# Letting the output matmuls of two token blocks take turns in the two halves of a PSUM bank

## The chip, the cores and the metric

The kernel runs on one core of one Trainium2 chip. The metric is the device time of one execution in microseconds; most executions of one kernel agree within 0.3%. A trace belongs to one profiled execution, whose span is some 2 us shorter than the timed execution (695.1 us of 696.8 us for the kernel before). It gives the start of every matmul; the ends of matmuls in it are modelled, so lengths and busy times of matmuls below carry that model, and spacings of starts don't.

## The reference

The first half is a short causal convolution along the tokens, with softmax weights of 7 taps per head. The second half is a two-layer network with a Swish activation. Only the second half matters here.

```python
# x: 32768 tokens x 192, w_in: 192 x 2048, w_out: 2048 x 192
def _moe_ref(x, w_in, w_out, beta):
    h = x @ w_in
    g = h * (1.0 / (1.0 + np.exp(-beta * h)))
    return (g @ w_out).astype(np.float32)
```

## The kernel before

Two halves of the batch are processed at once, one in partitions 0 to 63 and one in partitions 64 to 127. A step takes 512 tokens of each half. It has 16 rounds, and in one round TensorE does two things. It computes one group of 128 hidden features for the current step ("hidden", three pairs of matmuls), and it does one sixteenth of the output matmuls of the previous step ("output", eight pairs).

A *pair* is two matmuls, one per row half of the array (rows 0 to 63 and 64 to 127), which run at the same time. Each writes a bank of its own in PSUM, the memory that matmuls write and in which their sums add up. The stationary operand is loaded into the array first (LDWEIGHTS, listed as PEld); the moving operand then streams through it, column by column. For the output, the stationary operand is a 64 x 128 piece of the activations `g` (64 features of 128 tokens), and the moving operand is a 64 x 192 piece of `w_out_s`. Sixteen pairs (`fc` from 0 to 15) add up to one block of 128 tokens. Two blocks share a PSUM tile: block 0 (`b == 0`) lies in columns 0 to 191 of each bank, block 1 in columns 192 to 383. When both are done, VectorE (DVE) copies one bank, adds the other, and the result is stored.

```python
    def output(s, u):
        g = gs[s]
        nb = steps[s][2] // BLK
        per = 2 * nb
        for i in range(u * per, (u + 1) * per):
            blk, fc = divmod(i, NF)               # all 16 fc of one block, then the next block
            h, q = divmod(blk, nb)
            b = q % 2
            single = s == N_ST - 1 and h == 1 and q >= nb - 2
            if single:
                b = 0
            if fc == 0 and b == 0:
                state["po"] = psum_o.tile([128, 2, TOK], FP32, name="po")
            # ... (osb tile)
            for r in range(2):                    # the two row halves: one pair
                rows = slice(r * 64, (r + 1) * 64)
                nc.tensor.matmul(
                    po[:, r, b * D : (b + 1) * D],
                    g[rows, fc, h, q * BLK : (q + 1) * BLK],   # stationary
                    w_out_s[rows, fc, :],                      # moving
                    start=(fc == 0),
                    stop=(fc == NF - 1),
                )
            if fc == NF - 1 and (b == 1 or single):
                # ... copy po[:, 0], add po[:, 1], store
```

## Time and profile before

| | before |
|---|---|
| median of the timed runs | 697.0 us (3 runs, 696.14 to 697.85) |
| TensorE busy share of the span | 99% |
| ScalarE / VectorE busy share | 83% / 80% |
| start of one output pair to start of the next | 82.5 ns |
| start of one hidden pair to start of the next | 215.8 ns |

These are lines of the profile's page of the kernel before: the span, the busy time of each engine (share of the span, number of instructions), the chain of work that ended last by engine, and the costliest groups. A group's columns are the line, engine, operation, output<-inputs, shapes and count, then busy us and mean ns of one, then the idle time of the engine just before them.

```profile
span 695.1 us, 24857 instructions
...
PE 686.9 (99%) x11465; PEld 525.9 (76%) x11465; DVE 553.2 (80%) x935; ACT 578.7 (83%) x545; POOL 69.8 (10%) x83
...
PE 96%; DVE 3%; ACT 0%; issue 0%
...
L370 ACT ACTIVATE g<-ph,beta 128x1024 bf16<-128x1024 f32 (+1 forms) x528 | 571.8, 1088 | 97.0 <-PE ph L363 93.1
L410 PEld LDWEIGHTS <-g 64*128 64x128 bf16 x8192 | 368.9, 94 | 102.4 <-issue 0.2
L410 PE MATMUL po<-w_out_s,g 64*128 64x192 bf16 x8192 | 429.8, 243 | 0.0
L363 PE MATMUL ph<-ct,w_in_s 64*128 64x512 bf16 (+1 forms) x3168 | 425.5, 370 | 2.8 <-ACT g L370 1.4
```

TensorE (PE) is busy all the time and is 96% of the chain. The output matmuls have 0.0 us of idle time in front of them. A mean of 243 ns is the length of one matmul from its start to its modelled end. It is not the price of one, because matmuls overlap: 8,192 of 243 ns would be 1,991 us.

The windows view of the same kernel shows three stretches of the steady part. Each entry is the busy time in that stretch with the number of instructions; then come the granted clock, the DMA share and GB/s.

```profile
core 0: us, PE busy (x) PEld busy (x) DVE busy (x) ACT busy (x) POOL busy (x), PEclk, DMA share, GB/s
60.00:260.00 200.00, 200.00 (x3371) 152.88 (x3367) 175.60 (x297) 170.32 (x154) 30.68 (x34) 1.00 0.92 101
260.00:460.00 200.00, 200.00 (x3371) 152.88 (x3368) 162.70 (x279) 170.44 (x153) 0.00 (x0) 1.00 0.25 60
460.00:660.00 200.00, 200.00 (x3370) 152.88 (x3366) 152.37 (x257) 170.48 (x153) 0.00 (x0) 1.00 0.20 54
```

TensorE is busy in every nanosecond of 600 us at full clock. To learn the price of a pair one needs starts. The timeline of two rounds (start in us, busy us, engine, group, count) shows the rhythm:

```profile
start us, us, engine line op out<-in xcount [idle before <-releaser]
...
400.31 0.83 PE L363 MATMUL ph<-ct,w_in_s 64*128 64x512 bf16 x6
...
400.96 0.84 PE L410 MATMUL po<-w_out_s,g 64*128 64x192 bf16 x16
401.17 1.11 ACT L370 ACTIVATE g<-ph,beta 128x1024 bf16<-128x1024 f32 x1 [0.19 <-PE ph L363]
...
401.62 0.83 PE L363 MATMUL ph<-ct,w_in_s 64*128 64x512 bf16 x6
...
402.92 0.83 PE L363 MATMUL ph<-ct,w_in_s 64*128 64x512 bf16 x6
```

Hidden runs start at 400.31, 401.62 and 402.92 us: a round takes about 1.305 us. ScalarE (ACT) takes 1.11 us of it and then waits 0.19 us for TensorE, so ScalarE follows and does not lead. The starts of single matmuls are read from the trace's records. Around 400 us they are, for the output:

```
399649  399668   399731  399750   399814  399833   399896  399915  (ns)
```

Each two are a pair. The partner starts 19 ns after the first, and the next pair 63 or 64 ns after that. Between 60 and 550 us the mean from pair to pair is 82.50 ns over 5,242 spacings inside output runs (counted on each row half), and none of them is outside 82 to 83 ns. Hidden pairs have 215.84 ns. Three hidden and eight output pairs are 3 x 215.8 + 8 x 82.5 = 1,307 ns, which is the whole round.

### The profile page before, as it was taken

How to read it: one execution, taken by the hardware profiler on the slowest of the kernel's cores; microseconds unless marked ns; L12 is line 12 of the kernel's file. 1: busy time of each engine (PE TensorE's matmuls, PEld its weight loads, DVE VectorE, ACT ScalarE, POOL GpSimd, SP SyncE). 2: the span in 40 equal slices, each digit the busy share in tenths (PEclk: the TensorE clock that was granted, in tenths of full speed). 3: DMA queues.
4: the chain of work that ended last, by engine and by line, in shares of the span. 5: the costliest groups of instructions: out<-in, count | busy, mean ns of one | idle time of the engine just before them, and what ended most of it. 6: DMA issues, size and time to landing. Idle time of an engine off the chain costs nothing.

```text
span 695.1 us, 24857 instructions
## 1 busy us (share of the span) xinstructions
PE 686.9 (99%) x11465; PEld 525.9 (76%) x11465; DVE 553.2 (80%) x935; ACT 578.7 (83%) x545; POOL 69.8 (10%) x83
## 2 busy tenths in 40 slices
PE   8899999999999999999999999999999999999997
PEld 6767777777777777777777777777777777777777
DVE  6999999998777987777987777987778987777222
ACT  5898888888888888888888888888888888888881
POOL 6934455000000000000000000000000000000000
PEclk9999999999999999999999999999999999999999
DMA  9999999922232022322023222032123122111012
GB/s 175 146 160 160 169 177 171 138 62 70 54 65 71 27 68 72 47 70 70 26 70 71 49 70 69 26 71 70 48 72 55 41 70 71 48 48 48 25 48 70
DMA packets 181497, 54.57 MB, mean 79 GB/s; under 512 B 146432, under 2 KB 181072, under 8 KB 181392
## 3 DMA queue, kind: packets, MB, share of 16 engines
q0 software_dynamic: 98048, 14.89, 29.9%
q1 hardware_dynamic: 83296, 38.09, 23.6%
q8 instruction: 89, 1.46, 0.9%
q14 instruction: 16, 0.13, 0.1%
q10 hardware_dynamic: 48, 0.01, 0.0%
HBM read 28.98 MB, written 37.29 MB: 95 GB/s over the span
## 4 chain that ended last, share of the span: by engine, by line
PE 96%; DVE 3%; ACT 0%; issue 0%
PE po L410 48%; PE ph L363 46%; DVE ct L346 2%; DVE ct L344 1%; PE ph L204 1%; PE ph L249 0%; PE po L236 0%; PE po L208 0%; DVE w_in_s L149 0%; ACT g L370 0%; PE po L249 0%; DVE xt L314 0%; DVE osb L425 0%; DVE ct L300 0%; DVE osb L424 0%
## 5 line engine op out<-in xcount | busy, mean ns | idle before, releaser
L370 ACT ACTIVATE g<-ph,beta 128x1024 bf16<-128x1024 f32 (+1 forms) x528 | 571.8, 1088 | 97.0 <-PE ph L363 93.1
L410 PEld LDWEIGHTS <-g 64*128 64x128 bf16 x8192 | 368.9, 94 | 102.4 <-issue 0.2
L410 PE MATMUL po<-w_out_s,g 64*128 64x192 bf16 x8192 | 429.8, 243 | 0.0
L363 PE MATMUL ph<-ct,w_in_s 64*128 64x512 bf16 (+1 forms) x3168 | 425.5, 370 | 2.8 <-ACT g L370 1.4
L346 DVE SCALAR_TENSOR_TENSOR ct<-xt,cw,ct 128x512 bf16<-128x512 bf16 x558 | 380.4, 746 | 0.0
L363 PEld LDWEIGHTS <-w_in_s 64*128 64x128 bf16 x3168 | 162.4, 94 | 56.9 <-issue 3.6
L424 DVE COPY osb<-po 128x384 f32<-128x384 f32 x127 | 70.8, 558 | 126.3 <-PE po L410 120.2
L425 DVE TENSOR_TENSOR osb<-po,osb 128x384 f32<-128x384 f32 x129 | 71.5, 554 | 6.0 <-ACT osb L422 1.6
L95 POOL DMA_DIRECT2D xd<-in_x_dram x60 | 54.3, 906 | 47.8 <-DMA xd<-in_x_dram 43.5
L344 DVE TENSOR_SCALAR ct<-xt,cw 128x512 bf16<-128x512 bf16 x93 | 31.6, 393 | 0.0
L422 ACT COPY osb<-po 128x192 f32<-128x192 f32 x2 | 0.6, 318 | 9.9 <-PE po L410 9.9
L320 POOL TENSOR_TENSOR w_out_s<-w_out_raw,beta_r 128x768 bf16<-128x768 f32 x4 | 5.9, 1500 | 2.3 <-DMA w_out_raw<-in_moe_w_out_dram 2.3
L204 PE MATMUL ph<-zeros 128*128 128x512 bf16 x8 | 3.8, 627 | 1.3 <-DVE warm L132 1.3
L249 PE MATMUL po<-xt_145,diag 128*128 128x256 f32 x28 | 4.4, 296 | 0.0
L249 PEld LDWEIGHTS po<-xt_145,diag 128*128 128x128 f32 x28 | 3.6, 189 | 0.7 <-issue 0.6
L149 DVE COPY w_in_s<-w_in_s 64x1536 bf16<-64x1536 bf16 x4 | 2.7, 699 | 1.5 <-DMA w_in_s<-in_moe_w_in_dram 1.4
L184 POOL DMA_DIRECT2D w_out_raw<-in_moe_w_out_dram x4 | 3.1, 782 | 0.0
L249 PEld LDWEIGHTS ph<-xt_145,diag 128*128 128x128 f32 x14 | 2.6, 269 | 0.7 <-ACT xt_145 L270 0.6
L249 PE MATMUL ph<-xt_145,diag 128*128 128x256 f32 x14 | 3.1, 375 | 0.0
L204 PEld LDWEIGHTS <-zeros 128*128 128x128 bf16 x8 | 0.9, 130 | 2.5 <-issue 1.3
L142 POOL DMA_DIRECT2D w_in_s<-in_moe_w_in_dram x4 | 2.6, 667 | 0.8 <-POOLq L479 0.8
L261 ACT CAST ct<-po 128x256 bf16<-128x256 f32 x1 | 0.4, 372 | 2.8 <-PE po L249 2.8
(46 smaller groups left out, 27.7 us busy)
## 6 DMA issues: line engine op xcount, KB each, us to landing
out_dram<-osb SPq DMA_DIRECT2D x60, 384.0 KB, 3.0
xd<-in_x_dram POOLq DMA_DIRECT2D x54, 198.0 KB, 14.6
w_out_raw<-in_moe_w_out_dram POOLq DMA_DIRECT2D x4, 384.0 KB, 9.6
out_dram<-osb SPq DMA_DIRECT2D x7, 192.0 KB, 3.8
xd<-in_x_dram POOLq DMA_DIRECT2D x6, 192.0 KB, 14.0
x_83<-in_x_dram SPq DMA_DIRECT2D x4, 192.0 KB, 3.9
w_in_s<-in_moe_w_in_dram POOLq DMA_DIRECT2D x4, 192.0 KB, 7.9
xt<-xd SPq DMA_TRANSPOSE x30, 4.6
```

Of the source, the lines that this page charges most:

```text
L95: nc.gpsimd.dma_start(out=xd[r0:, :, h, :], in_=x_v[p, t0:t1, h, :].rearrange("t (c d) -> t c d", c=NG),)
L184: nc.gpsimd.dma_start(out=w_out_raw[:, c : c + 4, :], in_=w_out_v[:, c : c + 4, :])
L204: nc.tensor.matmul(pf[:, 0, :], zeros[:, 0:128], zeros, start=True, stop=True)
L249: nc.tensor.matmul(pv, diag[:, c, k, :], xt0[:, c, o : o + n], start=(k == 0), stop=(k == K - 1),)
L320: nc.gpsimd.tensor_tensor(w_out_s[:, c0 : c0 + n, :], w_out_raw[:, c0 : c0 + n, :], beta_r[:, c0 : c0 + n].unsqueeze(2).to_broadcast((128, ...
L344: nc.vector.tensor_scalar_mul(dst, src, scalar)
L346: nc.vector.scalar_tensor_tensor(out=dst, in0=src, scalar=scalar, in1=dst, op0=ALU.mult, op1=ALU.add)
L363: nc.tensor.matmul(ph[:, h, 0:n], w_in_s[rows, j, cols], cts[s][rows, j, 0:n], start=(j == 0), stop=(j == NG - 1),)
L370: nc.scalar.activation(gs[s][:, fc, :, 0:n], ph[:, :, 0:n], AF.Silu, scale=beta[:, fc : fc + 1])
L410: nc.tensor.matmul(po[:, r, b * D : (b + 1) * D], g[rows, fc, h, q * BLK : (q + 1) * BLK], w_out_s[rows, fc, :], start=(fc == 0), stop=(fc ...
L424: nc.vector.tensor_copy(dst, po[:, 0, cols])
L425: nc.vector.tensor_tensor(dst, po[:, 1, cols], dst, ALU.add)
```

## The change

Its evident intent is to separate successive accumulations. Before, each output matmul adds onto the columns that the matmul just before it in the same row half has written. With turns, block 0 and block 1 alternate, so a column is written again only every second pair. Successive pairs then also share the moving operand `w_out_s[rows, fc]`. `start` marks a matmul that begins a new sum; one without it adds. Because a PSUM bank now holds two open sums, only the first matmul of block 0 may have `start` set. The last two blocks of the program keep the old order, since they are copied and stored one by one.

```diff
--- before.py
+++ after.py
@@ -393,9 +393,14 @@
         nb = steps[s][2] // BLK
         per = 2 * nb
         for i in range(u * per, (u + 1) * per):
-            blk, fc = divmod(i, NF)
-            h, q = divmod(blk, nb)
-            b = q % 2
+            pair, rest = divmod(i, 2 * NF)
+            h, q = divmod(2 * pair, nb)
+
+            if s == N_ST - 1 and h == 1 and q == nb - 2:
+                b, fc = divmod(rest, NF)
+            else:
+                fc, b = divmod(rest, 2)
+            q += b
 
             single = s == N_ST - 1 and h == 1 and q >= nb - 2
             if single:
@@ -411,8 +416,9 @@
                     po[:, r, b * D : (b + 1) * D],
                     g[rows, fc, h, q * BLK : (q + 1) * BLK],
                     w_out_s[rows, fc, :],
-                    start=(fc == 0),
+                    start=(fc == 0 and b == 0),
                     stop=(fc == NF - 1),
+                    skip_group_check=True,
                 )
             if fc == NF - 1 and (b == 1 or single):
                 n_q = 1 if single else 2
```

## The prediction

> **What bounds the kernel now.** TensorE. The busy table gives PE 99% of the 695.1 us span, ACT 83%, DVE 80%; the chain of waits puts 96% on PE, 48% on output matmuls. The windows view has PE busy 200.00 of 200.00 us in three windows between 60 and 660 us, at granted clock 1.00. Matmuls overlap, so "busy" proves little; I read start times. In a steady round (timeline near 400 us) output matmuls come in pairs, one per row half: the partner starts 19 to 20 ns later, the next pair 63 to 64 ns after that, so a pair costs 82.5 ns; a hidden pair costs 215.8 ns. A round of 3 hidden and 8 output pairs is 3 x 215.8 + 8 x 82.5 = 1307 ns; rounds in the timeline start every 1.30 to 1.31 us. From 60 to 660 us no gap between output starts exceeds 64 ns, nor any other 197 ns: nothing waits.
>
> **Is there a stall to remove?** The change separates consecutive accumulations into the same PSUM columns: today each 192-column matmul adds onto what its row half wrote 82.5 ns earlier. A stall there would make the pair longer than its streaming. The Trainium skill, "TensorE: Matmul & The Clock Gate", section "Back-to-back issue gap", gives N/2.4 + 2.5 ns: 82.5 ns for N = 192, 215.8 ns for N = 512. The trace agrees to a tenth of a nanosecond. So accumulation costs nothing that turns could hide. Even if the 2.5 ns beyond streaming vanished from all 4,096 output pairs, it would be 10 us (1.5%); the hidden pairs show the same 2.5 ns, so I expect none.
>
> **What it removes, adds, moves.** No operation is removed or added. In the compiled orders DVE, ACT, POOL and SP match row by row in operation and wait; on PE only operands are reordered within each 32-pair group, and four waits (two for scaled output weights, two for the last activations) move later. Weight loads stay 8,192 of 94 ns, hidden behind the previous pair: the shared moving operand saves none, as g is the stationary one. A PSUM tile completes at the same place, so copies, adds and stores keep their times. The last two blocks keep their order, so the tail (last matmul at 690.7 us to the end) stays. The moved waits cost nothing: output matmuls show 0.0 us of idle.
>
> **Correctness.** Only block 0's first matmul has start set. The skill, "PSUM — Partial Sum Buffer", section "The four PSUM rules", says that this clears the written-bits of the whole bank, so block 1's first matmul overwrites. No run here shows it yet.
>
> **On the critical path.** All output matmuls are, but their change is estimated as 0 ns. Prediction: 697.0 us, range 695.0 to 699.2 (the three runs spread 696.1 to 697.9). Chances: faster by over 2% 0.01, within 2% 0.97, slower by over 2% 0.02.
>
> **What would show the steps right or wrong.** Right: output pairs 82.5 ns apart, rounds of 1.305 us, output matmul mean 243 ns, weight loads 94 ns, the other engines' groups unchanged, PE without idle. Wrong: pair spacing near 80 ns (a hidden accumulation cost) or above 83 ns (alternating columns or weight addresses cost something), or a new PE wait on DVE or ACT.
>
> **What would make it wrong.** A cost of switching columns inside a bank, or of weight reads that jump between token blocks: each nanosecond per pair adds 4 us, so 3.4 ns leaves the 2% band. A gain beyond 2% needs a pair under 79.1 ns, less than its 80 ns of streaming.

## The result

No change of the time could be measured.

| | before | after |
|---|---|---|
| median | 696.57 us (4 runs, 696.0 to 697.85) | 696.94 us (4 runs, 696.36 to 697.1) |
| ratio | 1 | 1.0001 (95% interval 0.9984 to 1.0019) |
| output pair to output pair, mean | 82.50 ns | 82.50 ns |
| hidden pair to hidden pair, mean | 215.84 ns | 215.82 ns |
| start of the last matmul to the end of the span | 4.37 us | 4.36 us |

The median before is 696.57 us here and 697.0 us above because a fourth run was added.

The lines of the page of the kernel after that answer to those above (its output matmuls stand at another line of the file, L415):

```profile
span 695.4 us, 24857 instructions
...
PE 687.2 (99%) x11465; PEld 527.5 (76%) x11465; DVE 552.5 (79%) x935; ACT 578.7 (83%) x545; POOL 69.8 (10%) x83
...
PE 94%; DVE 3%; DMA 1%; POOL 1%; issue 0%; ACT 0%; POOLq 0%
...
L370 ACT ACTIVATE g<-ph,beta 128x1024 bf16<-128x1024 f32 (+1 forms) x528 | 571.8, 1088 | 97.0 <-PE ph L363 93.0
L415 PEld LDWEIGHTS <-g 64*128 64x128 bf16 x8192 | 369.7, 94 | 101.4
L415 PE MATMUL po<-w_out_s,g 64*128 64x192 bf16 x8192 | 430.2, 243 | 0.0
L363 PE MATMUL ph<-ct,w_in_s 64*128 64x512 bf16 (+1 forms) x3168 | 426.0, 370 | 2.8 <-ACT g L370 1.4
```

The three stretches of the kernel after:

```profile
core 0: us, PE busy (x) PEld busy (x) DVE busy (x) ACT busy (x) POOL busy (x), PEclk, DMA share, GB/s
60.00:260.00 200.00, 200.00 (x3368) 153.31 (x3366) 174.98 (x296) 170.32 (x154) 31.02 (x35) 1.00 0.93 101
260.00:460.00 200.00, 200.00 (x3369) 153.31 (x3366) 162.72 (x279) 170.43 (x154) 0.00 (x0) 1.00 0.25 60
460.00:660.00 200.00, 200.00 (x3370) 153.26 (x3366) 152.42 (x258) 170.42 (x154) 0.00 (x0) 1.00 0.21 54
```

And its timeline:

```profile
400.61 0.83 PE L363 MATMUL ph<-ct,w_in_s 64*128 64x512 bf16 x6
...
401.26 0.84 PE L415 MATMUL po<-w_out_s,g 64*128 64x192 bf16 x16
401.48 1.11 ACT L370 ACTIVATE g<-ph,beta 128x1024 bf16<-128x1024 f32 x1 [0.19 <-PE ph L363]
...
401.92 0.83 PE L363 MATMUL ph<-ct,w_in_s 64*128 64x512 bf16 x6
...
403.23 0.83 PE L363 MATMUL ph<-ct,w_in_s 64*128 64x512 bf16 x6
```

The starts of single output matmuls in this stretch, again from the trace's records:

```
401262  401282   401344  401364   401427  401447   401509  401529  (ns)
```

Counts are the same, and means, idle times and the period of a round (400.61, 401.92, 403.23 us) are the same too. Pairs are 82 or 83 ns apart as before. The chain has 94% instead of 96% on TensorE. This difference lies in the first 15 us: after, the chain runs through 8 us of loading the input weights there, and before through TensorE's first work. A second profile of the changed kernel has 96% again, so it is no effect of the change.

### The profile page after: what moved, and what is told of

Read it like the earlier page. It is cut to its first block, busy times and chain, and to the rows that moved or that the text cites. A ratio compares the mean times of both kernels' runs of the same rounds, so it can differ in the third digit from the quotient of the medians.

```text
span 695.4 us, 24857 instructions
## 1 busy us (share of the span) xinstructions
PE 687.2 (99%) x11465; PEld 527.5 (76%) x11465; DVE 552.5 (79%) x935; ACT 578.7 (83%) x545; POOL 69.8 (10%) x83
## 4 chain that ended last, share of the span: by engine, by line
PE 94%; DVE 3%; DMA 1%; POOL 1%; issue 0%; ACT 0%; POOLq 0%
PE po L415 48%; PE ph L363 46%; DVE ct L346 2%; DMA w_in_s<-in_moe_w_in_dram 1%; DVE ct L344 1%; DVE w_in_s L149 0%; POOL x1b L117 0%; DVE xt L314 0%; DVE osb L431 0%; DVE ct L300 0%; POOL w_in_s L142 0%; POOL sel L158 0%; POOL sel L167 0%; DVE osb L430 0%; DVE xt L311 0%
## 5 line engine op out<-in xcount | busy, mean ns | idle before, releaser
L415 PEld LDWEIGHTS <-g 64*128 64x128 bf16 x8192 | 369.7, 94 | 101.4
L415 PE MATMUL po<-w_out_s,g 64*128 64x192 bf16 x8192 | 430.2, 243 | 0.0
```

Source lines behind the costliest of these rows:

```text
L415: nc.tensor.matmul(po[:, r, b * D : (b + 1) * D], g[rows, fc, h, q * BLK : (q + 1) * BLK], w_out_s[rows, fc, :], start=(fc == 0 and b == 0 ...
```

## The experiments

**Theory 1** is the one of the prediction: matmuls already follow each other at the pace of their streaming, adding onto freshly written columns costs nothing, and so there is nothing for turns to hide. **Theory 2** is a rival that the equal times alone don't exclude: accumulation does cost something, and the change hides it, but its own side effects (alternating columns or alternating weight addresses) cost as much. **Rival 3** says that something other than the stream of matmuls sets the time, so that gains in the output matmuls don't show.

The first four kernels ran together in five rounds.

### The changed kernel again, with more rounds

There is no edit.

> The changed kernel as it is, timed in more rounds. Theory 1 (the stream of matmuls already runs at its streaming rate, so there is no stall to hide): ratio to before within 0.3% of 1, output pairs 82.5 ns apart. Theory 2 (the change hides an accumulation stall, and what it adds, alternating columns or weight addresses, costs as much): the same here; the two next runs tell them apart.

The median was 696.56 us, before 696.53 us, ratio 0.9998 (0.9986 to 1.0011), and the pair 82.5 ns. The result is confirmed to about 0.1%.

### No accumulation at all

```diff
-                    start=(fc == 0),
+                    start=True,
                     stop=(fc == NF - 1),
+                    skip_group_check=True,
```

> The kernel before, but every output matmul has start set, so none adds onto what is in PSUM; the result is wrong on purpose. Theory 1: output pairs stay 82.5 ns apart and the time is that of before within 0.3%. Theory 2: without accumulation the pair falls towards its 80 ns of streaming, up to 2.5 ns less on each of 4,096 pairs, so up to 10 us (1.5%) faster.

The median was 696.53 us, ratio 0.9999 (0.9986 to 1.0011). Mean pair spacing was 82.50 ns over 5,242 spacings, as before. The result is wrong, as meant: the relative error of 0.969 is what remains if only the last of 16 partial sums is kept, about the root of 15/16, 0.968. So accumulation was really off. Lines of its page:

```profile
span 694.8 us, 24857 instructions
...
PE 686.7 (99%) x11465; PEld 527.4 (76%) x11465; DVE 552.3 (79%) x935; ACT 578.8 (83%) x545; POOL 70.9 (10%) x83
...
L410 PE MATMUL po<-w_out_s,g 64*128 64x192 bf16 x8192 | 430.2, 243 | 0.0
```

The group of output matmuls has the same 430 us, mean and idle time as with accumulation. So no accumulation stall shows in the kernel before, and Theory 2 loses its premise. One way out is left here: if setting `start` cost exactly what adding costs, this run would look the same. The next two runs change how soon a column is written again and keep nearly all matmuls adding.

### Columns in turn, weights in the old order

```diff
-                    po[:, r, b * D : (b + 1) * D],
+                    po[:, r, (0 if single else fc % 2) * D : (1 if single else fc % 2 + 1) * D],
...
-                    start=(fc == 0),
+                    start=(fc == 0 and b == 0),
                     stop=(fc == NF - 1),
+                    skip_group_check=True,
```

> The order of weights of before (block after block), but successive matmuls write alternately into the two halves of the bank; the result is wrong on purpose. Theory 1: pairs 82.5 ns, time within 0.3% of before. Theory 2: with the accumulation stall hidden and no jump in the weight addresses, faster by up to 1.5% if the weight order is what pays it back; slower than before if the column change is the added cost.

The median was 697.0 us, ratio 1.0004 (0.9991 to 1.0016), and the pair 82.50 ns. Wrong (relative error 0.99). The output matmuls on its page:

```profile
L410 PE MATMUL po<-w_out_s,g 64*128 64x192 bf16 x8192 | 429.6, 243 | 0.0
```

### Weights in turn, columns in the old order

The edit is to the changed kernel:

```diff
-                    po[:, r, b * D : (b + 1) * D],
+                    po[:, r, (0 if single else rest // NF) * D : (1 if single else rest // NF + 1) * D],
```

> The order of weights of the changed kernel (two blocks in turn), but 32 matmuls in a row write one half of the bank and the next 32 the other, as before; the result is wrong on purpose. Theory 1: pairs 82.5 ns, time within 0.3% of before. Theory 2: slower than before if jumping weight addresses are the added cost, by as much as the columns-only run is faster.

The median was 697.2 us, ratio 1.0008 (0.9995 to 1.0022), and the pair 82.51 ns in the mean (single spacings 81 to 84 ns). Wrong (relative error 1.00). The output matmuls on its page:

```profile
L415 PE MATMUL po<-w_out_s,g 64*128 64x192 bf16 x8192 | 430.3, 243 | 0.0
```

Together with the kernels before and after these two fill a table of two by two, weights in either order by columns in either order. All four cells have pairs of 82.50 or 82.51 ns and ratios to before within 0.08% of 1. No gain and cost cancel here, because neither shows by itself: a wait on freshly written columns would have shortened the pair of the run with columns in turn, whose columns rest for 165 ns and not 82.5. Theory 2 falls.

### Output matmuls of 160 instead of 192 columns

This kernel and the two with 96 columns ran together in three rounds, with one execution of the last kernel of this section beside them; the two with 32 columns ran later, also in three rounds. The first matmul of each block keeps 192 columns, so that every column is written once.

```diff
-                    po[:, r, b * D : (b + 1) * D],
+                    po[:, r, b * D : b * D + (D if fc == 0 else 160)],
                     g[rows, fc, h, q * BLK : (q + 1) * BLK],
-                    w_out_s[rows, fc, :],
+                    w_out_s[rows, fc, 0 : (D if fc == 0 else 160)],
```

> The kernel before, with 160 instead of 192 columns in every output matmul except the first of each block; wrong on purpose. Theory 1 (the pace of matmuls is the time): pairs near 160/192 of the streaming time plus 2.5 ns, 69.2 ns, rounds near 1.20 us instead of 1.305, total down by 3,840 pairs x 13.3 ns = 51 us to about 645 us. Rival 3 (something other than the stream of matmuls sets the time, so nothing done to output matmuls shows): above 680 us.

The median was 648.13 us against 696.52 us for before, ratio 0.9305 (0.9287 to 0.9323). Most pairs (5,245 of 5,656 spacings) were 69 or 70 ns apart, in the mean 69.2 ns, which is the expected spacing; nearly all others are the 192-column first pairs at 82 or 83 ns. The page and the groups by shape:

```profile
span 647.8 us, 24857 instructions
...
PE 637.6 (98%) x11465; PEld 476.9 (74%) x11465; DVE 545.6 (84%) x935; ACT 577.9 (89%) x545; POOL 70.7 (11%) x83
```

```profile
L410 PE MATMUL po<-w_out_s,g 64*128 64x160 bf16 x7680 | 358.5, 229 | 1.8 <-issue 1.8
L410 PE MATMUL po<-w_out_s,g 64*128 64x192 bf16 x512 | 67.2, 243 | 0.1
```

The gain of 48.4 us is a little under the estimate of 51 us. In the profiled run, 1.8 us of the difference is one pause before an output matmul for which the profile shows no cause ("issue"); the rest is not resolved. Rival 3 falls: a gain of 13.3 ns per pair reaches the total almost in full, so a gain from turns would have been seen. A tenth of a nanosecond per pair would be 0.4 us in all, which is below what these rounds resolve; for that the spacings themselves are the better witness.

### Output matmuls of 96 columns, in both orders

Here the same column is written again after about half the time. The edits are as above with 96, once to the kernel before and once to the changed kernel.

> The kernel before with 96 columns in the output matmuls, so that each adds onto what its row half wrote about half as long ago (42.5 ns if streaming still sets the pair); wrong on purpose. In the last stretch, where only output matmuls run, theory 1 expects the same pair spacing here as in the run with turns. If accumulation has a latency that shows only at short distances, the pair here is longer than with turns. The total should be limited by ACT (busy 579 us) or DVE (busy 553 us), about 560 to 600 us, so the spacing and not the total decides.

> The changed kernel with 96 columns in the output matmuls; wrong on purpose. Theory 1: pair spacing in the last stretch equal to the block order's run within 1 ns, total within 1% of it. A latency of accumulation that shows at short distances: a shorter pair here.

The medians were 584.49 us (block order) and 583.32 us (turns), ratios to before 0.8392 (0.8376 to 0.8408) and 0.8372 (0.8341 to 0.8403). Over the steady part (60 to 550 us), 42 or 43 ns is the spacing of 5,740 of 6,328 pairs in block order and of 5,723 of 6,313 with turns (most of the rest are the 192-column first pairs). So adding again after 42.5 ns still costs nothing.

In the last stretch, where only output matmuls run, the averages do differ: 49.1 ns per pair in block order and 45.3 ns with turns, over 100 pairs, seven of them wide in each run. A reader of averages would have found that turns are faster. The single starts tell otherwise. In block order one gap of 392 ns where its neighbours have 23 falls into these 100 pairs; (4,910 - 369) / 100 leaves 45.4 ns. The timeline of the block order's run (columns as before) shows what ended this pause:

```profile
569.21 3.15 ACT L370 ACTIVATE g<-ph,beta 128x1024 bf16<-128x1024 f32 x3
...
571.03 1.20 PE L410 MATMUL po<-w_out_s,g 64*128 64x96 bf16 x46
...
572.41 3.77 PE L410 MATMUL po<-w_out_s,g 64*128 64x96 bf16 x160 [0.19 <-ACT g L370]
```

The first piece ends 46 matmuls in, which is just before `fc` 15 of the last step's first block (16 matmuls belong to the step before), and the next piece was released by ScalarE (the view's 0.19 us counts from the modelled end of the matmul before, the gap above from start to start): the last activation (the third of the ACT line) had ended at 572.36 us. With turns that activation is needed only after 30 pairs of the last step and not after 15, and no pause is there. This is one true effect of turns, a later need of the last activations, once per program and 0.4 us long. In the kernel before it is not there to be saved: at 82.5 ns per pair the 15 pairs take 1.24 us, and `fc` 15 comes, by this count, at 681.35 us, 0.57 us after the last activation ended (680.78 us).

The totals are limited elsewhere now. The page of the block order:

```profile
PE 553.7 (95%) x11465; PEld 378.4 (65%) x11465; DVE 542.8 (93%) x935; ACT 537.8 (92%) x545; POOL 69.9 (12%) x83
...
DVE 69%; PE 19%; ACT 6%; issue 5%; ACTq 0%
```

And of turns:

```profile
PE 558.3 (96%) x11465; PEld 383.4 (66%) x11465; DVE 542.8 (93%) x935; ACT 540.0 (93%) x545; POOL 69.9 (12%) x83
...
DVE 69%; PE 24%; issue 5%; ACT 2%; ACTq 0%
```

These are the busy line and the first line of the chain. VectorE is 69% of the chain in both. TensorE still reads 95% and 96% busy, although it no longer sets the time.

### Output matmuls of 32 columns, in both orders

> The kernel before with 32 columns in the output matmuls (192 in the first of each block); wrong on purpose. Streaming would give 32/96 of the 40 ns of the 96-column run plus 2.5 ns, about 16 ns per pair, so issuing or weight loading should set the pair. Theory 1: the pair spacing is the same in both orders. A latency of accumulation that 42.5 ns still hid: longer pairs here than with turns, by up to a factor of two if the latency alone sets them. The total should be near that of the 96-column runs, 575 to 585 us, as DVE bounds those (93% busy, 69% of the chain).

> The changed kernel with 32 columns in the output matmuls; wrong on purpose. Theory 1: pair spacing as in the block order within 1 ns, total within 1% of it. An accumulation latency: shorter pairs here.

The medians were 581.68 us and 581.42 us, ratios 0.8349 (0.8324 to 0.8374) and 0.8353 (0.833 to 0.8376). The most frequent pair spacing was 25 ns in both, 4,618 of 6,368 spacings in block order and 4,731 of 6,352 with turns. Over all pairs that begin with 32 columns and are under 60 ns apart, the mean is 25.56 ns in block order and 25.51 ns with turns. The output matmuls by shape, first block order, then turns:

```profile
L410 PE MATMUL po<-w_out_s,g 64*128 64x32 bf16 x7680 | 185.9, 173 | 7.4 <-issue 6.8 <-ACT g L370 0.6
L410 PE MATMUL po<-w_out_s,g 64*128 64x192 bf16 x512 | 66.9, 243 | 13.5 <-DVE osb L425 13.5
```

```profile
L415 PE MATMUL po<-w_out_s,g 64*128 64x32 bf16 x7680 | 186.1, 173 | 6.5 <-issue 6.4
L415 PE MATMUL po<-w_out_s,g 64*128 64x192 bf16 x512 | 44.3, 244 | 12.0 <-DVE osb L431 12.0
```

The narrow matmuls are alike in length (173 ns) and in busy time (186 us). The larger busy time of the 512 wide ones in block order (66.9 against 44.3 us) is no price of accumulation: busy time counts overlapping matmuls once, and with turns the two blocks' wide first matmuls stand next to each other and overlap (as estimates from one length of 243 ns: 256 pairs of 243 + 20 ns are 67 us, 128 groups of 243 + 20 + 82.5 ns are 44 us). Each run also has 12.0 to 13.5 us of waits for VectorE to free a PSUM tile. So a column may be added to again after 25 ns, while matmuls of 173 ns by the profile's model are under way, and the order of blocks makes no difference beyond 0.05 ns.

### start set in both blocks

This undoes one safeguard of the changed kernel.

```diff
-                    start=(fc == 0 and b == 0),
+                    start=(fc == 0),
```

> The changed kernel with start set in both blocks' first matmul, as the kernel before has it. The time should be that of before. If the start of block 1 clears the written-bits of the whole bank, block 0's second matmul overwrites its first, and block 0 of each pair loses the first of 16 partial sums: a wrong result. If start clears only the columns that it writes, the result is right.

One run took 696.87 us, and its pairs were 82.50 ns apart. The result was wrong, with a relative error of 0.1756. If half of the blocks lose one of 16 about equal and unrelated partial sums, the estimate is the root of 1/2 x 1/16, 0.177. This fits the statement in the Trainium skill, "PSUM — Partial Sum Buffer", section "The four PSUM rules", that such a start clears the written-bits of the whole bank: block 0's second matmul then overwrites its first. The changed condition on `start` is therefore needed. It costs no time that shows: the pairs are 82.50 ns apart in this run and in the changed kernel.

## Why the prediction was right

The prediction was 697.0 us with a range of 695.0 to 699.2 us; the median measured was 696.94 us. That they lie within 0.06 us is chance: single runs of the kernel before spread over 1.85 us. What was predicted is the equality, and its mechanism held:

- *TensorE bounds the kernel, and the pace of pairs is its price.* Shown by the run with 160 columns: 13.3 ns less per pair took 48.4 us away. The prediction's rule, 4 us per nanosecond and pair, was somewhat high: 48.4 us over 13.3 ns is 3.6 us for the 3,840 narrowed pairs, where 3.8 us was to be expected.
- *There is no accumulation stall to hide.* Before the runs this was argued from the agreement of 82.5 ns with N/2.4 + 2.5 ns. (82.5 and 215.8 ns are estimates worked out from that formula; the trace alone gives the same line, since (215.84 - 82.50) ns over 320 columns is 0.4167 ns per column, with 2.5 ns left over.) It is now shown: with accumulation switched off the pair stayed at 82.50 ns and the time at ratio 0.9999. The prediction also took comfort from the same 2.5 ns in the hidden pairs. That could not decide anything, because hidden matmuls accumulate too (their `start` is set for the first of three pairs only), so a cost of adding could have sat in both.
- *The order itself costs nothing.* The prediction named a cost of switching columns or of jumping weight addresses as what could make it wrong. Each was run alone, and neither cost anything (82.50 and 82.51 ns).
- *Nothing else moves, and the moved waits cost nothing.* Weight loads stayed at 8,192 of 94 ns, the output matmuls at 243 ns. ScalarE's and VectorE's groups kept their counts, and their means stayed within 1% for activations, convolution updates, copies and adds; only the convolution's small first-tap group went from 393 to 386 ns. The tail stayed within 0.01 us. The later wait for the last activations saved 0.4 us only where 96 columns had made TensorE faster, as told above.
- *Correctness by one start per bank* held, and the run with two starts showed that it was needed.
- One point was weaker than it sounded. The prediction used the formula of the section "Back-to-back issue gap" as if it were the page's last word. The same section calls it the gap of an isolated matmul and gives other figures, about 81 ns at 128 columns and 131 ns at 512, for streams with weight loads. This trace, a stream with a weight load per matmul, agrees with the formula on each row half and not with those figures (nor does it if both matmuls of a pair are counted: half of 215.8 ns is 107.9 ns at 512 columns). The trace carried the argument; the page alone would not have.

No version that beats both kernels came out of the experiments. The correct ones are equal, and the faster ones leave out work.

## What to carry to other kernels

Before reordering matmuls to avoid a suspected stall, measure the spacing of their starts and compare it with the streaming time: a spacing that is already at that estimate (here 82.5 ns) suggests that nothing is left to hide, whatever the busy share says. A run with the suspected cause switched off shows it, even if its result is wrong. Where a gain and a cost could cancel, run each half of the change alone. An average over a short stretch can contain one pause with another cause, so look at the single spacings. If two sums share a PSUM bank, set start only in the first matmul of the bank; with start in both, the result here was wrong by 0.1756.

## What the Trainium skill lacked or had wrong

- "TensorE: Matmul & The Clock Gate" does not say whether a matmul that adds onto columns written just before pays for it. Here it paid nothing at re-use after 82.5, 42.5 and 25 ns: spacings were the same with turns at all three widths and, at the first, without accumulation too.
- The same page, "Back-to-back issue gap", gives sustained figures of about 81 ns per matmul at 128 columns and 131 ns at 512, and says that the formula N/2.4 + 2.5 ns under-counts small matmuls in streams with weight loads. In these runs, with a weight load for each matmul, pairs on two row halves were 215.8 ns apart at 512 columns, 82.5 at 192, 69.2 at 160 and 42.5 at 96. The formula gives, as estimates, 215.8, 82.5, 69.2 and 42.5 ns. No run here has 128 columns.
- The same page, "Wait — 56ns, not 53.3ns?", says that start-to-start never drops below about 25 ns. Here it was 25 ns per pair at 32 columns (starts 20 and 5 ns apart in turn), so two matmuls on different row halves start within it; the floor seems to hold per row half, which no run here separates further.
- The same page, "Part 3: Packing small matmuls — row/col tiling", shows row tiles starting about 4 ns apart. Here the partner started 19 to 20 ns after the first in the steady part of the kernel before, and 2 to 4 ns after it once TensorE had paused: behind the 392 ns gap of the 96-column block order, and at the end of the kernel before, behind a gap of 168 ns. The pair spacing was the same either way, 42 to 43 ns at 96 columns and 82 to 83 ns at 192. Why the offset stays at 19 to 20 ns until a pause was not tested.
- "PSUM — Partial Sum Buffer", "The four PSUM rules": nothing wrong was found; the whole-bank effect of start fits the run with start in both blocks, with a relative error of 0.1756 against an estimate of 0.177.
